# Routing order and filler products at the first expert of a two-stage mixture-of-experts kernel

## The chip, the cores and the metric

One core of a Trainium2 chip runs the whole program as one launch. The metric is device time in microseconds (us) of that launch, lower is better; the times given are medians of several runs on one chip, and the rows come from one further execution that was profiled.

## The reference, cut to what matters

The reference is an attention layer, a first mixture-of-experts layer and a second one (3072 tokens of 512 values, 8 experts, hidden size 1024). The change touches only the second:

```
logits = x @ w_gate                      # 3072 x 8
for idx in argsort(-logits.flatten()):   # best (token, expert) pair first
    tok, e = idx // 8, idx % 8
    if assigned[tok] >= 0 or counts[e] >= 384: continue
    assigned[tok] = e; counts[e] += 1
for e in range(8):
    h = relu(x[assigned == e] @ w1[e])   # 384 rows, 512 -> 1024
    out[assigned == e] = h @ w2[e]       # 1024 -> 512
```

Every expert ends with exactly 384 tokens, but who gets which token depends on all the experts that filled up earlier.

## The kernel before, in words

The expert stages of the second layer are `phase_d` (L911 on); they begin at about 287 us of the profile. The order in which the experts are worked on is found on the chip. One **choice** (`Route2.phase`, L774) finds the next expert to fill: a search in five steps (`NSTEP`) for the logit threshold, each step made of a comparison on VectorE (`p_g`, L801), a count on TensorE (`rt_ps`, L808 for the first choice, L810 for the later ones), a short chain on VectorE (L819 to L822), a sum over partitions on TensorE (L824) and the new threshold (L826). Then come the assignment (L834 to L844), a count (L841), the expert's number `p_ei` (L853, which the weights' load on SyncE waits for) and positions (L857 to L868). **The update** (`Route2.update`, L872) takes the filled expert and the assigned tokens out of the logits (L875 to L878); the next choice begins with it. **The list** (`Route2.list`, L879) turns positions into the 384 row numbers `p_ix` of the expert (L882 to L890 on VectorE and ScalarE, L896 or L899 on TensorE, L906).

With `p_ix` GpSimd gathers the rows: `gather` (L937) issues three indirect DMAs of 128 rows (L941). `fetch` (L917) loads the weights as four 1 MB chunks from SyncE's queue (for the first expert two of them from GpSimd's). `conv` (L920) splits a quarter of a chunk into a high part (ScalarE cast, L925) and a low part (subtraction, L934, on GpSimd; the first four on VectorE). `xT` (L949) turns 128 gathered rows: four TensorE transposes (L952), a cast on ScalarE and a subtraction on VectorE (both L955). `L1` (L956) makes the hidden values: for each of 8 blocks `f`, four groups of three 384-column products (L963 to L965), then ReLU (L968) and the low part (L969). `L2` (L974) makes the result: for each of 3 blocks `b`, eight groups of three 512-column products (L980 to L982), a copy (L985) and the indirect store (L987, issued by GpSimd). So an expert is 56 groups of three products, called **pieces** here: pieces 1 to 32 are L1, 33 to 40, 41 to 48 and 49 to 56 the blocks of L2.

All engines work through their instructions in the order in which the program was written, and that order comes from a planner at the end of `phase_d` that runs when the program is built. It keeps a clock `now`, in modelled us, and a clock `dve` for VectorE. A piece of L1 moves `now` by 0.522, a piece of L2 by 0.7 (what `yield` gives back). The route and the list are generators, too: each step adds its modelled VectorE time to `dve` (`busy`), and the next step is due 0.1 after that (0.25 from the second expert on). Between two pieces `try_thread` (L1013) runs a step that is due, lists first; `housekeeping` (L1037), asked only after an even number of pieces, issues a gather, a fetch or a conversion; `xts_step` (L1050) issues a turn once `now` is 4.5 us past the gather (one more us for each later block) and 34 pieces or more of the running expert are out:

```
if route[0] is None and route[2]<7 and (route[2] in routed if route[2] else 0 in listed): R.update(); busy(1.25); start_route(route[2]+1)
if (curp>=0 or xts.get(0,3)==3 or now[0]<gath_t[0]+HOLD) and try_thread(): continue
h=housekeeping() if hk or cur is None else False
if xts_step(): continue
```

`routed` holds the choices whose search and positions are done, `listed` those whose list is done. So before the change the update and the next choice follow as soon as a choice is routed, with the list's steps among them; only after the first choice (number 0) do they wait for its list. Choice 1 is made while expert 0 is worked on, choice 2 from the second half of expert 0 on.

`warm` (L487) issues products of a constant 128x128 matrix with 512 constant columns (L489), whose result nobody reads. Thirteen of them stand behind the first list (L909). `R.psum()` (L763) is the one PSUM tile of the route, `rt_ps`.

Of the kernel before, what the change touches and what calls it, by code (L numbers as in the profile page):

```python
# [6 lines left out]
F32=mybir.dt.float32; BF=mybir.dt.bfloat16; F32R=mybir.dt.float32r; I32=mybir.dt.int32; U32=mybir.dt.uint32  # L7
# [479 lines left out]
def warm(nc,st,p,n):  # L487

    for _ in range(n): nc.tensor.matmul(p,st['ones_b'],st['it32'].rearrange("p s c->p (s c)")[:,0:512],start=True,stop=True)  # L489
# [421 lines left out]
def phase_d(nc,tc,ctx,I,st,out,R,W,wk,ps,cp):  # L911
# [24 lines left out]
    def busy(x): dve[0]=max(dve[0],now[0])+x  # L936
# [12 lines left out]
    def xT(p,b):  # L949
        if b==0: S[p]['xh']=wk.tile([128,4,CAP],F32R,name="dxh",bufs=1); S[p]['xl']=wk.tile([128,4,CAP],F32R,name="dxl",bufs=1)  # L950
        q=ps.tile([128,512],F32,name="dh_ps",bufs=3).rearrange("p (d c)->p d c",d=4); x=S[p]['x'][b]
        for d in range(4): T.transpose(q[:,d,:],x[:,128*d:128*d+128],ident)  # L952
        c=slice(128*b,128*b+128); h=S[p]['xh'][:,:,c]
        busy(0.72)
        A.copy(h,q); V.tensor_tensor(S[p]['xl'][:,:,c],q,h.bitcast(F32),op=OP.subtract)  # L955
    def L1(p,f):  # L956
        s=S[p]
        if f==0: s['hh']=wk.tile([128,8,CAP],F32R,name="dhh",bufs=1); s['hl']=wk.tile([128,8,CAP],F32R,name="dhl",bufs=1)
        wh,wl=s['w'][f//4]
        q=ps.tile([128,512],F32,name="dh_ps",bufs=3)[:,0:CAP]  # L960
        for d in range(4):
            c=slice(512*d+128*(f%4),512*d+128*(f%4)+128)
            T.matmul(q,wh[:,c],s['xh'][:,d,:],start=(d==0),stop=False)  # L963
            T.matmul(q,wh[:,c],s['xl'][:,d,:],start=False,stop=False)  # L964
            T.matmul(q,wl[:,c],s['xh'][:,d,:],start=False,stop=(d==3))  # L965
            if d<3: yield 0.522
        h=s['hh'][:,f,:]
        A.activation(h,q,AF.Relu)  # L968
        def low(s=s,f=f,q=q,h=h): V.scalar_tensor_tensor(s['hl'][:,f,:],q,0.0,h.bitcast(F32),op0=OP.max,op1=OP.subtract)  # L969
        defer.append((now[0]+0.522+0.5,low))  # L970
        yield 0.522
    def flush(t=1e9):
        while defer and defer[0][0]<=t: busy(0.6); defer.pop(0)[1]()
    def L2(p,b):  # L974
# [16 lines left out]
    def expert(p):  # L991
        for f in range(8): yield from L1(p,f)
        for b in range(3): yield from L2(p,b)


    route=[None,0.0,0]
    pend=[]
    lists=[]
    rdy={}
    routed=[]; listed=[]  # L1000
    def step(th):

        try:
            lat,dur=next(th[0])
        except StopIteration: return False
        busy(lat); th[1]=dve[0]+(0.25 if curp>0 else 0.1); th.append(dur) if len(th)==3 else th.__setitem__(3,dur)
        return True
    def start_route(ph):
        route[0]=R.phase(ph); route[2]=ph; step(route)
# [3 lines left out]
    def try_thread():  # L1013
        for th in lists+[route]:
            if th[0] is not None and now[0]>=th[1]:
                now[0]+=th[3]
                if not step(th):
                    ph=th[2]; th[0]=None
                    if th is route:
                        routed.append(ph); pend.append(ph)  # L1020
                    else:
                        lists.remove(th); listed.append(ph)
                    if pend and not lists:
                        ph=pend.pop(0); l=[R.list(ph),now[0],ph]; lists.append(l); step(l)
                return True
        return False
# [11 lines left out]
    def housekeeping():  # L1038

        q=curp+1  # L1040
        if q==7 and q not in gath_t and q in listed and xts.get(curp)==3: gather(q); gath_t[q]=max(pool[0],now[0]); pool[0]=gath_t[q]+3.1; xts[q]=0; return True
        if curp>=0 and cur is not None and conv_step(curp,(0,0,0,0)): return True
        if q>7: return False
        if q not in fetch_t and q in routed and conved.get(curp,16)==16:
            fetch(q); fetch_t[q]=now[0]; conved[q]=0; return True
        if q not in gath_t and q in listed: gather(q); gath_t[q]=max(pool[0],now[0]); pool[0]=gath_t[q]+3.1; xts[q]=0; return True
        if xts.get(q,3)<3 and 33<=npc<=45: return False
        if cur is None and xts.get(q,0)<3 and conved.get(q,0)>=8: return False
        return conv_step(q,(0,0,18,34) if cur is not None else (0,0,0,0))
    def xts_step():  # L1050
        q=curp+1
        if q<=7 and xts.get(q,3)<3 and now[0]>=gath_t[q]+4.5+1.0*xts[q] and (cur is None or npc>=34+4*xts[q]):
            xT(q,xts[q]); xts[q]+=1; now[0]+=0.45; return True
        return False
    hk=True; HOLD=3.0
    while True:
        flush(now[0])
        if route[0] is None and route[2]<7 and (route[2] in routed if route[2] else 0 in listed): R.update(); busy(1.25); start_route(route[2]+1)
        if (curp>=0 or xts.get(0,3)==3 or now[0]<gath_t[0]+HOLD) and try_thread(): continue
        h=housekeeping() if hk or cur is None else False  # L1060
        if xts_step(): continue
        if cur is not None:
            if npc==32 and conved[curp]<12 or npc==36 and conved[curp]<16:
                hk=True
                if not h: now[0]+=0.3
                continue
            try: now[0]+=next(cur); npc+=1; hk=npc%2==0
            except StopIteration: cur=None
            if cur is not None: continue
            if curp==7: break  # L1070
        if cur is None:
            q=curp+1
            if xts.get(q,0)==3 and conved.get(q,0)>=8:
                curp=q; cur=expert(q); npc=0; continue
            if not h: now[0]+=0.3
# [4 lines left out]
def program(nc,tc,I,out,dbg=None):  # L1080
    with ExitStack() as ctx:
# [34 lines left out]
        ps=ctx.enter_context(tc.tile_pool(name="c_ps",reuse_waits="tile",bufs=2,space=PSUM))  # L1116
        R=Route2(nc,tc,cp,wk,ps,I,st)
        phase_d(nc,tc,ctx,I,st,out,R,W,wk,ps,cp)

# [15 lines left out]
```

## Time and profile before

| | us |
|---|---|
| median of 3 runs (lowest, highest) | 638.8 (638.35, 639.43) |
| the profiled execution, its own time | 643.75 |
| its span, first to last instruction | 642.1 |
| TensorE busy in the span | 588.6 (92%) |
| mean granted clock, share of 2.4 GHz | 0.946 |

The time of the profiled execution is what a row's change is set against; it is 4.95 us above the median of the unprofiled runs. In a row of a timeline the first number is the start in us from the span's beginning, the second how long the instruction, or a run of equal ones, took; in brackets stands how long the engine sat idle before it and what it waited for. In a table by stretches `PEclk` is the granted TensorE clock as a share of 2.4 GHz.

### The profile page before, as it was taken

What the parts mean: (1) busy time and instruction counts of PE and PEld (TensorE: products, weight loads), DVE (VectorE), ACT (ScalarE), POOL (GpSimd) and SP (SyncE); (2) the same over time, 40 slices, a digit from 0 to 9 for tenths busy, and PEclk for the clock granted to TensorE, in tenths of its full rate; (3) what the DMA queues carried; (4) which work ended last, traced back from release to release, by engine and by line L of the source; (5) the groups of instructions that cost most, each with busy time, mean ns of one, the idle gap of its engine ahead of it and who ended that gap; (6) DMA issues with size and microseconds to landing.
All of it is one profiled execution on the core that took longest, in us unless ns stands there. A gap on an engine that the chain in (4) does not pass through costs nothing.

```text
span 642.1 us, 13487 instructions
## 1 busy us (share of the span) xinstructions
PE 588.6 (92%) x4848; PEld 465.5 (73%) x4848; DVE 426.4 (66%) x1618; ACT 328.0 (51%) x740; POOL 364.9 (57%) x401
## 2 busy tenths in 40 slices
PE   7799999898799999983599899999999999999994
PEld 3567667666677777753388588797888879798983
DVE  4678888888878996847857447676777767642110
ACT  5789989784367766400341432543517245363610
POOL 2565555432446879610471653875939488496931
PEclk9899999998899999985779879999999999999998
DMA  8999794282099778000712704518082451854000
GB/s 321 404 380 382 252 350 149 91 306 100 29 366 316 238 248 278 20 10 3 244 69 97 264 1 178 184 62 284 17 294 67 177 171 44 316 195 150 33 17 33
DMA packets 48644, 114.62 MB, mean 179 GB/s; under 512 B 3937, under 2 KB 4705, under 8 KB 48576
## 3 DMA queue, kind: packets, MB, share of 16 engines
q1 hardware_dynamic: 40016, 88.60, 38.3%
q0 software_dynamic: 6208, 20.39, 9.4%
q10 hardware_dynamic: 2352, 4.76, 2.1%
q8 instruction: 39, 0.64, 0.4%
q14 instruction: 29, 0.24, 0.1%
HBM read 99.26 MB, written 14.88 MB: 178 GB/s over the span
## 4 chain that ended last, share of the span: by engine, by line
PE 40%; issue 5%; POOL 3%; DVE 3%; DMA 1%; ACT 1%; POOLq 0%; DVEq 0%; ACTq 0%
PE dh_ps L963 7%; PE dh_ps L964 7%; PE dh_ps L965 6%; PE dz_ps L980 5%; PE dz_ps L982 5%; PE dz_ps L981 5%; POOL wl L934 2%; PE dh_ps L952 2%; DMA xg<-xrows,p_ix 1%; PE rt_ps L810 1%; POOL out_dram L987 1%; DVE p_g L801 1%; PE rt_ps L808 1%; ACT dxh L955 0%; ACT wh L925 0%
## 5 line engine op out<-in xcount | busy, mean ns | idle before, releaser
L934 POOL TENSOR_TENSOR wl<-wraw,wh 128x512 fp32r<-128x512 f32 x124 | 155.6, 1290 | 14.3 <-ACT wh L925 13.9
L963 PE MATMUL dh_ps<-dxh,wh 128*128 128x384 f32 x256 | 94.2, 368 | 2.5 <-ACT dxh L955 2.5
L964 PE MATMUL dh_ps<-dxl,wh 128*128 128x384 f32 x256 | 89.8, 351 | 0.4 <-DVE dxl L955 0.3
L965 PE MATMUL dh_ps<-dxh,wl 128*128 128x384 f32 x256 | 89.0, 348 | 0.0
L980 PE MATMUL dz_ps<-wh,dhh 128*128 128x512 f32 x192 | 78.8, 410 | 0.0
L982 PE MATMUL dz_ps<-wh,dhl 128*128 128x512 f32 x192 | 76.0, 396 | 0.0
L981 PE MATMUL dz_ps<-wl,dhh 128*128 128x512 f32 x192 | 76.0, 396 | 0.0
L925 ACT CAST wh<-wraw 128x512 fp32r<-128x512 f32 x128 | 73.5, 619 | 2.8 <-DMA wraw<-in_w1b_dram 2.8
L968 ACT ACTIVATE dhh<-dh_ps 128x384 fp32r<-128x384 f32 x64 | 31.5, 493 | 84.4 <-PE dh_ps L965 73.3
L987 POOL DMA_INDIRECT out_dram<-dz,io x24 | 24.6, 1025 | 86.8 <-ACT dz L985 84.7
L969 DVE SCALAR_TENSOR_TENSOR dhl<-dh_ps,dhh 128x384 fp32r<-128x384 f32 x64 | 35.5, 555 | 56.0 <-ACT dhh L968 55.9
L133 ACT ACTIVATE p_e<-s_sb,nm 128x118 f32<-128x118 f32 x192 | 59.9, 389 | 0.0
L985 ACT COPY dz<-dz_ps 128x512 f32<-128x512 f32 x24 | 14.1, 587 | 85.4 <-PE dz_ps L982 60.3
L963 PEld LDWEIGHTS dh_ps<-dxh,wh 128*128 128x128 f32 x256 | 50.4, 197 | 3.1 <-ACT dxh L955 2.8
L505 POOL TENSOR_TENSOR wl<-wraw,wh 128x1024 fp32r<-128x1024 f32 (+1 forms) x18 | 37.4, 2106 | 26.6 <-ACT wh L504 26.6
L504 ACT CAST wh<-wraw 128x1024 fp32r<-128x1024 f32 (+1 forms) x56 | 48.9, 932 | 6.3 <-DMA wraw<-in_w1a_dram 6.0
L964 PEld LDWEIGHTS dh_ps<-dxl,wh 128*128 128x128 f32 x256 | 50.3, 196 | 2.3 <-DVE dxl L955 2.2
L965 PEld LDWEIGHTS dh_ps<-dxh,wl 128*128 128x128 f32 x256 | 50.0, 195 | 0.0
L115 POOL COPY VV<-wraw 24x1024 f32<-24x1024 f32 x24 | 24.0, 1032 | 45.6 <-ACT wraw L114 45.6
L505 DVE TENSOR_TENSOR wl<-wraw,wh 128x1024 fp32r<-128x1024 f32 (+1 forms) x38 | 45.0, 1222 | 5.9 <-ACT wh L504 5.9
L127 DVE CUSTOM_DVE_ANT_0 s_sb<-s_ps,cst 128x118 f32<-128x118 f32 x192 | 41.9, 275 | 9.9 <-PE s_ps L123 7.7
L941 POOL DMA_INDIRECT xg<-xrows,p_ix x24 | 23.3, 973 | 38.5 <-DVE rrow L875 24.3
(340 smaller groups left out, 1375.0 us busy)
## 6 DMA issues: line engine op xcount, KB each, us to landing
wraw<-in_w1b_dram SPq DMA_DIRECT2D x16, 1024.0 KB, 6.7
wraw<-in_w2b_dram SPq DMA_DIRECT2D x14, 1024.0 KB
VV<-in_v_dram SPq DMA_DIRECT2D x16, 780.0 KB, 11.7
wraw<-in_w2a_dram SPq DMA_DIRECT2D x12, 1024.0 KB, 9.2
wraw<-in_w1a_dram SPq DMA_DIRECT2D x10, 1024.0 KB
kt<-in_k_dram SPq DMA_DIRECT2D x16, 384.0 KB, 6.3
qd<-in_q_dram SPq DMA_DIRECT2D x16, 384.0 KB, 6.0
wraw<-in_vt_dram SPq DMA_DIRECT2D x8, 768.0 KB, 8.8
```

The costliest lines, as they stand in the source:

```text
L127: V.tensor_tensor_reduce(out=sb[:,j,:],in0=p[j%2][:,j//2,0:118],in1=mk,scale=-0.125,scalar=3e38,op0=OP.add,op1=OP.min,accum_out=nm[:,j:j+1])
L133: A.activation(pe[:,j,:],sb[:,j,:],AF.Exp,bias=nm[:,j:j+1],scale=-1.0)
L504: (hi.tensor_copy if hi else nc.scalar.copy)(h[:,c],t[:,c])
L505: (lo or nc.vector).tensor_tensor(l[:,c],t[:,c],h[:,c].bitcast(F32),op=OP.subtract)
L925: A.copy(h[:,c],t[:,c])
L934: eng.tensor_tensor(l[:,c],t[:,c],h[:,c].bitcast(F32),op=OP.subtract)
L963: T.matmul(q,wh[:,c],s['xh'][:,d,:],start=(d==0),stop=False)
L964: T.matmul(q,wh[:,c],s['xl'][:,d,:],start=False,stop=False)
L965: T.matmul(q,wl[:,c],s['xh'][:,d,:],start=False,stop=(d==3))
L980: T.matmul(q,s['hh'][:,f,c0],wh[:,c],start=(f==0),stop=False)
L981: T.matmul(q,s['hh'][:,f,c0],wl[:,c],start=False,stop=False)
L982: T.matmul(q,s['hl'][:,f,c0],wh[:,c],start=False,stop=(f==7))
```

## The change

Three edits, all in `phase_d`:

- `L1`: for the first expert (`p` is 0) the planner counts 0.65 instead of 0.522 for each piece of the blocks `f` 0 and 1, that is for pieces 1 to 8. No instruction is added.
- A new list `laid` is filled together with `listed`. After choice 1 the update and choice 2 now wait until list 1 is done (`route[2] in laid`), as they did after choice 0. Choices from 2 on are as before.
- `xts_step`: behind the three turns of the first expert's rows (`q==0`) stand 3, 3 and 2 products of constants into `rt_ps`.

```diff
-        q=ps.tile([128,512],F32,name="dh_ps",bufs=3)[:,0:CAP]
+        q=ps.tile([128,512],F32,name="dh_ps",bufs=3)[:,0:CAP]; t=0.522 if p or f>1 else 0.65
...
-            if d<3: yield 0.522
+            if d<3: yield t
...
-        defer.append((now[0]+0.522+0.5,low))
-        yield 0.522
+        defer.append((now[0]+t+0.5,low))
+        yield t
...
-    routed=[]; listed=[]
+    routed=[]; listed=[]; laid=[]
...
-                        lists.remove(th); listed.append(ph)
+                        lists.remove(th); listed.append(ph); laid.append(ph)
...
-            xT(q,xts[q]); xts[q]+=1; now[0]+=0.45; return True
+            xT(q,xts[q]); xts[q]+=1; now[0]+=0.45
+            if q==0: warm(nc,st,R.psum(),(3,3,2)[xts[q]-1])
+            return True
...
-        if route[0] is None and route[2]<7 and (route[2] in routed if route[2] else 0 in listed): R.update(); busy(1.25); start_route(route[2]+1)
+        if route[0] is None and route[2]<7 and (route[2] in routed if route[2]>1 else route[2] in laid): R.update(); busy(1.25); start_route(route[2]+1)
```

## Rows read from the trace of the kernel before

**Rows 1.** The page's part 2, granted TensorE clock in 40 slices of the span

```profile
PEclk9899999998899999985779879999999999999998
```

**Rows 2.** Busy us by stretch: PE, PEld, DVE, ACT, POOL; then PEclk, DMA share, GB/s

```profile
315.00:320.00 5.00, 2.38 (x14) 1.41 (x14) 3.89 (x7) 2.68 (x5) 2.52 (x4) 1.00 0.77 217
320.00:325.00 5.00, 5.00 (x27) 4.54 (x28) 1.81 (x7) 2.58 (x6) 5.00 (x5) 0.57 0.80 282
325.00:330.00 5.00, 5.00 (x32) 4.42 (x31) 2.41 (x8) 1.52 (x3) 1.86 (x2) 0.75 0.02 8
...
355.00:360.00 5.00, 5.00 (x42) 3.90 (x39) 2.18 (x9) 2.57 (x5) 2.31 (x3) 1.00 1.03 395
...
365.00:370.00 5.00, 3.12 (x14) 2.40 (x13) 3.26 (x10) 3.35 (x7) 4.97 (x5) 0.51 0.13 52
...
400.00:405.00 5.00, 5.00 (x49) 3.74 (x48) 2.19 (x9) 0.44 (x1) 2.61 (x3) 1.00 1.02 374
```

**Rows 3.** Timeline of PE, the first expert's turns and its first product

```profile
310.11 4.81 PE L489 MATMUL rt_ps<-it,ones_b 128*128 128x512 bf16 x13
314.82 0.66 PE L952 MATMUL dh_ps<-cb,xg 128*128 128x128 f32 x4
316.38 0.66 PE L952 MATMUL dh_ps<-cb,xg 128*128 128x128 f32 x4 [0.91 <-DMA xg<-xrows,p_ix]
317.79 0.66 PE L952 MATMUL dh_ps<-cb,xg 128*128 128x128 f32 x4 [0.75 <-DMA xg<-xrows,p_ix]
319.13 0.45 PE L963 MATMUL dh_ps<-dxh,wh 128*128 128x384 f32 x1 [0.67 <-ACT dxh L955]
```

**Rows 4.** Timeline of PE, products of the first expert at either clock

```profile
320.96 0.52 PE L963 MATMUL dh_ps<-dxh,wh 128*128 128x384 f32 x1
...
327.61 0.34 PE L965 MATMUL dh_ps<-dxh,wl 128*128 128x384 f32 x1
...
332.11 0.34 PE L965 MATMUL dh_ps<-dxh,wl 128*128 128x384 f32 x1
...
333.13 0.34 PE L964 MATMUL dh_ps<-dxl,wh 128*128 128x384 f32 x1
```

**Rows 5.** Timeline of PE, second half of expert 0 and all of expert 1's L1

```profile
343.67 0.40 PE L980 MATMUL dz_ps<-wh,dhh 128*128 128x512 f32 x1
...
362.18 0.40 PE L982 MATMUL dz_ps<-wh,dhl 128*128 128x512 f32 x1
363.92 0.66 PE L952 MATMUL dh_ps<-cb,xg 128*128 128x128 f32 x4 [1.35 <-DMA xg<-xrows,p_ix]
...
368.79 0.69 PE L963 MATMUL dh_ps<-dxh,wh 128*128 128x384 f32 x1 [1.84 <-ACT dxh L955]
...
393.06 0.39 PE L980 MATMUL dz_ps<-wh,dhh 128*128 128x512 f32 x1
```

**Rows 6.** Timeline of DVE, list 1 and choice 2 among its steps

```profile
349.19 0.19 DVE L883 TENSOR_SCALAR st_ps<-st_ps 128x24 int32<-128x24 int32 x1
...
350.62 0.36 DVE L780 TENSOR_REDUCE st_ps<-Lm 128x24 f32<-128x192 f32 x1
...
355.61 0.64 DVE L906 SCALAR_TENSOR_TENSOR p_ix<-st_ps,l_oc 32x3 int32<-32x3 f32 x4
```

**Rows 7.** Timeline of POOL, the gather of expert 1's rows

```profile
357.08 1.00 POOL L987 DMA_INDIRECT out_dram<-dz,io  x1 [4.76 <-ACT dz L985]
358.39 1.00 POOL L941 DMA_INDIRECT xg<-xrows,p_ix  x1 [0.30 <-issue]
```

**Rows 8.** Timelines of POOL and PE, from expert 1 to expert 2

```profile
402.87 1.01 POOL L941 DMA_INDIRECT xg<-xrows,p_ix  x1 [2.08 <-DVE p_ix L906]
...
408.68 0.66 PE L952 MATMUL dh_ps<-cb,xg 128*128 128x128 f32 x4
409.10 0.47 PE L980 MATMUL dz_ps<-wh,dhh 128*128 128x512 f32 x1
...
413.20 0.42 PE L963 MATMUL dh_ps<-dxh,wh 128*128 128x384 f32 x1
```

## The prediction

> **What bounds the kernel now.** I read the page's 40 slices first. TensorE is busy nearly everywhere and its clock is near full, with dips around slices 19 to 24 [rows 1], and that is where the changed code runs. The table by stretches of 5 us then says what is wrong there: the clock is full from 315 to 320 while TensorE is busy for only 2.38 of 5 us, 0.57 and 0.75 of full in the next two stretches although TensorE is busy throughout, and again 0.51 from 365 to 370 [rows 2]. So two things cost time: products at half clock at the start of each of the first two experts, and a hole between them. From 380 us on TensorE works without a gap to the last result, so what the first two experts lose or win should reach the end.
>
> The timeline of TensorE explains the first dip. Thirteen products of constants bring the clock up; then come three turns, each waiting for its gather, and the expert's first product at 319.13 [rows 3]. In that stretch TensorE was more than half idle, and from about 320.7 on the products stand 0.32 us apart (1.2 GHz) instead of 0.177 (2.4 GHz) until 327.61 [rows 4].
>
> The hole: expert 0's last product starts at 362.18, the first turn for expert 1 waits for the gathered rows until 363.92, expert 1 begins at 368.79 and its L1 lasts to 393.06, 24.27 us, much of it at half clock [rows 5, 2]. The gather is late for two reasons. List 1 is stretched: between its second instruction (349.19) and its last (355.61) VectorE also does the update and begins choice 2 [rows 6]. And on GpSimd's queue the gather stands behind the store of expert 0's second block, which waits for that block: 357.08, then the gather at 358.39, though `p_ix` was complete at 356.25 [rows 6, 7]. One expert later the same hand-over works: gather at 402.87, turns from 408.68 inside the old expert's L2, next expert at 413.20, no hole [rows 8].
>
> **The change, part by part.** *Products of constants.* Eight of 512 columns; between the turns TensorE waits anyway. At full clock each takes at most 0.26 us (expert 0's L2, 72 products of the same width and four small blocks, took 18.9 us [rows 5]); the thirteen, mostly at half clock, took 0.37 each [rows 3]. The gaps are wide enough: the first turn ends at 315.48, three products end by 316.26, the next turn came at 316.38; the last turn ends at 318.45, two products end by 318.97, the first L1 product came at 319.13 [rows 3]. Cover: the wait for gather, cast and subtraction; without it they would cost 2.1 us at the one and 3 us at the other price. Benefit: if TensorE stays busy enough to keep its clock, the stretch 320.96 to 327.61 (17 products, one L810 block, one L824) takes 17 x 0.177 + 0.67 + 0.13 = 3.8 us instead of 6.65. The 0.67 is 332.11 to 333.13 less two product spacings [rows 4]; the 0.13 is an estimate from the same timeline. **Gain 2.85**; bounds 0 (the clock falls all the same) and 2.85.
>
> *The planner's 0.65.* No instruction; it moves route steps earlier in TensorE's order. I walked the planner's clocks through expert 0 with it: the five counts come after pieces 3, 9, 14, 19, 25 instead of 4, 10, 15, 21, 26, and choice 1 ends after piece 39 instead of 40. Could TensorE then wait for VectorE at a count? The gaps between sum and next count stay at 3 pieces (1.6 us) or more, and threshold and comparison take 1.3 us, so I count 0, at most 0.3 for each of five counts.
>
> *List before update.* The list's steps now go out after pieces 39, 40, 43, 44 and end after 46; before, 40, 41, 46, 47 and 50. Piece 48 carries the second block's store, so at 46 the gather goes on GpSimd's queue **ahead** of it. Update and choice 2 come behind the list on VectorE; queued behind them are only choice 2's counts, which the planner places later too: after pieces 53 and 56. The store now waits behind three gather issues (some 3.9 us of GpSimd); nobody needs it soon. In `p_ix` time: 356.25 less three pieces of 0.7 is about 354.1 against 358.39 now, so the gather is 4.3 us earlier relative to TensorE's work. A gather took from 358.39 to just before 363.92, 5.5 us [rows 5, 7]; landing is then about 15.9 us behind the start of L2, and the planner puts the turns after pieces 53, 53 and 54, 15.8 us behind it. So they fit inside L2, with a wait of 0 to 2 us; I take 0.5.
>
> Expert 0's L2 lasted 18.9 us (343.67 to 362.58). Add three turns at 0.42 [rows 8] and one more count (0.67): 20.8, plus 0.5 wait, 21.3 to expert 1's start, against 25.12 now [rows 5]. **Gain 3.8**; bounds 2.3 and 4.4.
>
> *Expert 1 at full clock.* With no hole nothing lowers the clock (expert 2 started so [rows 8]). 96 x 0.177 + 3 x 0.67 + 4 x 0.13 is 19.5 us instead of 24.27. **Gain 4.75**; bounds 0 (a hole remains) and 4.75.
>
> *Later.* By the walk, choice 2 ends after piece 35 of expert 1, as before, with both clocks in the same relation, so the order from there on is the old one and the gain is carried to the end.
>
> Sum: 2.85 + 3.8 + 4.75 = 11.4. Against the profiled execution: 643.75 - 11.4 = 632.35 (span 630.7); the unprofiled median lies 4.95 lower, so 627.4.
>
> One thing speaks against the moved gather. It now goes out while the weights are still coming: DMA share 1.03 from 355 to 360 [rows 2], instead of at their end. The Trainium skill (DMA: Bandwidth & Descriptors, "Issuing engines are not separate DMA queues") says that transfers issued from different engines run on the same 16 DMA engines and interleave; by that the gather and the weights delay each other. 0.79 MB of rows at 395 GB/s is an estimate of 2.0 us, which would make the sum 9.9. The hand-over in rows 8 shows turns 5.8 us behind a gather that also began while the share was 1.02 (400 to 405 [rows 2]), so I stay with 0.5.
>
> **Rivals.** *The clock falls all the same.* For: it fell after a stretch that held turns, which the change keeps. Against: eight products fill the waits. Then 2.85 is lost, the order is unchanged: 630.3. Chance 0.2.
>
> *The list ends one piece later.* Its last two due times meet `now` exactly: 0.6 + 0.1 is one piece of 0.7, 1.3 + 0.1 is two. If rounding breaks a tie, it ends after 47, the gather is asked for after 48, behind the store, as now. Then only the first gain is left: 636. Chance 0.06.
>
> *Choice 2 never catches up (slower).* Place: update and choice 2 behind list 1. If choice 2 ends after piece 38 instead of 35 of expert 1, its gather falls behind piece 48's store and the hole comes again, at 4.4 + 4.75 = 9 us a time. It decides from the second such hand-over; choices follow each other without slack, so all five up to expert 6 would have it: 638.8 - 11.4 + 5 x 9 = 672. Against: the walk gives piece 35. Chance 0.06.
>
> *The gather and the weights collide* by the 2 us above or more, in part of the hand-over: 630. Chance 0.08.
>
> **How the numbers follow.** Forecast as summed: chance 0.6, 627.4. About 0.2% (1.3 us) is what a measurement can tell from no change. Faster takes in the forecast, the fallen clock, the collision and most of the late list: 0.91; slower 0.06; same 0.03. The range: below, the sum of the upper bounds (12.0) and some 2 us for cold stretches that differ between executions, 624.5; above, the fallen clock with the collision's 2 us and a little, 633.5. That leaves out the late list and the slow case, and some of the unprofiled spread.
>
> **What would show it.** Right: the clock stays full from 314 us to the end; L810 first comes after nine L1 products; L2 of expert 0 begins near 340.8; the gather is issued by GpSimd ahead of the second block's store, near 351; three turns lie inside expert 0's L2; expert 1 begins near 362 and its L1 lasts 19.5 us. Wrong: clock at 0.5 behind 320; the gather behind the store; L952 waiting over 2 us; a hole at a later hand-over.

## The result, and the profile after

| | before | after |
|---|---|---|
| median of 11 runs each, us (lowest, highest) | 639.43 (637.9, 642.82) | 633.83 (632.26, 637.2) |
| the profiled execution, its own time, us | 643.75 | 636.16 |
| its span, us | 642.1 | 634.4 |

The changed kernel is faster: ratio 0.9908, 95% interval 0.9886 to 0.993; the medians lie 5.6 us apart. The forecast was 627.4 us with a range of 624.5 to 633.5. So the direction is right and the size is half of what was forecast. The time lies just above the range. Of all the runs told of here one lies far off, 794.89 us at a mean granted clock of 0.646 (old order with products, e5), and no ratio below includes it.

The first view of after is the page's second part, the granted clock of TensorE in 40 slices [rows 1]:

```profile
PEclk8689999979799999995599999999999999999998
```

The dips that stood behind slice 20 are gone. The one in slices 19 and 20 lies ahead of the first expert's turns, where [rows 1] have it too. In slices 1 to 3, 9 and 11, which the change doesn't touch, the clock is lower than in [rows 1]. Next the same view as [rows 2], busy us by stretch of 5 us (PE, PEld, DVE, ACT, POOL, then the granted clock, the DMA share, GB/s):

```profile
315.00:320.00 5.00, 4.51 (x22) 2.17 (x21) 4.83 (x11) 2.30 (x5) 4.33 (x6) 0.91 0.84 251
320.00:325.00 5.00, 4.18 (x30) 2.72 (x29) 2.58 (x6) 3.06 (x6) 2.40 (x2) 1.00 0.93 295
325.00:330.00 5.00, 5.00 (x38) 4.42 (x39) 3.35 (x13) 3.48 (x7) 5.00 (x5) 1.00 0.32 125
...
355.00:360.00 5.00, 4.62 (x20) 3.38 (x18) 2.94 (x7) 2.15 (x4) 4.12 (x7) 1.00 1.05 398
360.00:365.00 5.00, 3.94 (x33) 3.08 (x34) 2.91 (x9) 2.92 (x6) 4.30 (x4) 1.00 0.34 132
365.00:370.00 5.00, 5.00 (x47) 4.19 (x45) 3.46 (x11) 3.88 (x8) 3.81 (x6) 1.00 0.15 56
```

From 320 us on the clock is full, through the first expert's L1 and through the hand-over to the second, where [rows 2] had 0.57, 0.75 and 0.51. TensorE's timeline shows what stands between the turns now [rows 3]:

```profile
313.71 3.62 PE L489 MATMUL rt_ps<-it,ones_b 128*128 128x512 bf16 x11 [0.22 <-issue]
317.70 0.66 PE L952 MATMUL dh_ps<-cb,xg 128*128 128x128 f32 x4 [0.37 <-DMA xg<-xrows,p_ix]
318.19 0.81 PE L489 MATMUL rt_ps<-it,ones_b 128*128 128x512 bf16 x3
319.12 0.66 PE L952 MATMUL dh_ps<-cb,xg 128*128 128x128 f32 x4
319.61 0.81 PE L489 MATMUL rt_ps<-it,ones_b 128*128 128x512 bf16 x3
320.72 0.66 PE L952 MATMUL dh_ps<-cb,xg 128*128 128x128 f32 x4 [0.29 <-DMA xg<-xrows,p_ix]
321.21 0.59 PE L489 MATMUL rt_ps<-it,ones_b 128*128 128x512 bf16 x2
322.05 0.45 PE L963 MATMUL dh_ps<-dxh,wh 128*128 128x384 f32 x1 [0.24 <-ACT dxh L955]
...
343.67 0.47 PE L980 MATMUL dz_ps<-wh,dhh 128*128 128x512 f32 x1
...
360.59 0.66 PE L952 MATMUL dh_ps<-cb,xg 128*128 128x128 f32 x4 [0.97 <-DMA xg<-xrows,p_ix]
...
363.49 0.18 PE L824 MATMUL rt_ps<-p_any,ones_b 128*128 128x1 bf16 x1 [0.46 <-DVE p_any L822]
...
365.96 0.45 PE L963 MATMUL dh_ps<-dxh,wh 128*128 128x384 f32 x1
...
385.76 0.39 PE L980 MATMUL dz_ps<-wh,dhh 128*128 128x512 f32 x1
```

The products are hidden as forecast: they take the place of most of the idle time that stood ahead of the second and third turn (0.91 and 0.75 us before, none and 0.29 now) and of the first product (0.67 before, 0.24 now). The lower rows are the hand-over. The first turn now starts 16.92 us after L2's start at 343.67, inside L2, and it waits 0.97 us for its gathered rows. Inside the hand-over the sum over partitions of choice 2 (L824) waits 0.46 us for VectorE. Expert 1 begins at 365.96 with no idle time in front of it, where [rows 5] had 1.84 us. GpSimd's timeline answers to [rows 7], VectorE's to [rows 6]:

```profile
354.36 1.03 POOL L941 DMA_INDIRECT xg<-xrows,p_ix  x1 [2.16 <-DVE rrow L875]
...
358.42 1.08 POOL L987 DMA_INDIRECT out_dram<-dz,io  x1 [0.21 <-issue]
```

```profile
348.44 0.19 DVE L883 TENSOR_SCALAR st_ps<-st_ps 128x24 int32<-128x24 int32 x1
...
353.44 0.64 DVE L906 SCALAR_TENSOR_TENSOR p_ix<-st_ps,l_oc 32x3 int32<-32x3 f32 x4
...
355.32 0.36 DVE L780 TENSOR_REDUCE st_ps<-Lm 128x24 f32<-128x192 f32 x1
```

The gather stands ahead of the second block's store on GpSimd's queue, 4.06 us ahead of it, where it stood behind. On VectorE the list is done (353.44) before choice 2 begins (355.32). From its second instruction to its last it takes 5.00 us, against 6.42 in [rows 6].

So each step of the forecast is in the trace; the hand-over, 22.29 us from 343.67 to 365.96, is 1.0 us longer than forecast. Where is the other half of the gain? The sum of the three stretches that were forecast (expert 0's L1, the hand-over, expert 1's L1) fell from 73.93 us [rows 3, 5] to 385.76 - 322.05 = 63.71, by 10.2. That is near the forecast's 11.4. All expert stages, from the first use of the logits (L727 on VectorE, 287.02 us before, 289.79 after) to the end of the span, fell from 355.05 to 344.57, by 10.5. Of that, 2.8 were lost again because the stages began later, in phases that the change doesn't touch. The profiled execution of before lay above all 11 runs of the same kernel in the table, though (643.75 against a median of 639.43). The experiments had to tell whether its cold stretches were ordinary.

### The profile page after: what moved, and what is told of

The parts are those of the page before. It is cut to its first block, busy times and chain, and to the rows that moved or that the text cites. A ratio compares the mean times of both kernels' runs of the same rounds, so it can differ in the third digit from the quotient of the medians.

```text
span 634.4 us, 13501 instructions
## 1 busy us (share of the span) xinstructions
PE 585.2 (92%) x4853; PEld 462.7 (73%) x4856; DVE 424.2 (67%) x1618; ACT 328.4 (52%) x740; POOL 363.6 (57%) x401
## 4 chain that ended last, share of the span: by engine, by line
PE 41%; issue 4%; POOL 3%; DVE 3%; DMA 2%; ACT 0%; POOLq 0%; DVEq 0%; ACTq 0%
PE dh_ps L963 7%; PE dh_ps L964 6%; PE dh_ps L965 6%; PE dz_ps L980 6%; PE dz_ps L981 6%; PE dz_ps L982 6%; POOL wl L934 2%; PE dh_ps L952 2%; DMA xg<-xrows,p_ix 2%; PE rt_ps L810 1%; DVE p_g L801 1%; PE rt_ps L808 1%; POOL out_dram L987 1%; PE dx_ps L896 0%; PE rt_ps L824 0%
## 5 line engine op out<-in xcount | busy, mean ns | idle before, releaser
L963 PE MATMUL dh_ps<-dxh,wh 128*128 128x384 f32 x256 | 91.3, 357 | 0.2 <-ACT dxh L955 0.2
L964 PE MATMUL dh_ps<-dxl,wh 128*128 128x384 f32 x256 | 87.2, 340 | 0.3 <-DVE dxl L955 0.3
L965 PE MATMUL dh_ps<-dxh,wl 128*128 128x384 f32 x256 | 86.4, 338 | 0.0
L980 PE MATMUL dz_ps<-wh,dhh 128*128 128x512 f32 x192 | 78.8, 410 | 0.0
L964 PEld LDWEIGHTS dh_ps<-dxl,wh 128*128 128x128 f32 x256 | 48.2, 188 | 1.9 <-DVE dxl L955 1.8
L963 PEld LDWEIGHTS dh_ps<-dxh,wh 128*128 128x128 f32 x256 | 48.4, 189 | 1.0 <-ACT dxh L955 0.7
L965 PEld LDWEIGHTS dh_ps<-dxh,wl 128*128 128x128 f32 x256 | 48.1, 188 | 0.0
L505 DVE TENSOR_TENSOR wl<-wraw,wh 128x1024 fp32r<-128x1024 f32 (+1 forms) x38 | 42.8, 1164 | 5.3 <-ACT wh L504 5.3
```

The source lines that it names most:

```text
L505: (lo or nc.vector).tensor_tensor(l[:,c],t[:,c],h[:,c].bitcast(F32),op=OP.subtract)
L980: T.matmul(q,s['hh'][:,f,c0],wh[:,c],start=(f==0),stop=False)
```

## The experiments

In all of them three distances are read from TensorE's timelines, from the first L963 or L980 row of each: **L1 of 0** is from expert 0's first product to its L2, **hand-over** from there to expert 1's first product, **L1 of 1** from there to its L2. **Stages** is from the L727 row to the end of the span, to about 0.05 us, since a span is given to a tenth.

| kernel | L1 of 0 | hand-over | L1 of 1 | stages | their start |
|---|---|---|---|---|---|
| before, the profile of the forecast | 24.54 | 25.12 | 24.27 | 355.05 | 287.0 |
| before, second (e1) | 22.89 | 24.59 | 21.71 | 350.08 | 288.7 |
| before, third (e7) | 22.94 | 24.48 | 21.79 | 350.10 | 288.1 |
| after, first | 21.62 | 22.29 | 19.80 | 344.57 | 289.8 |
| after, second (e8) | 21.60 | 22.36 | 19.79 | 344.49 | 286.8 |
| after, third (e11) | 21.60 | 22.12 | 19.79 | 344.25 | 287.5 |
| products alone (e2) | 21.58 | 24.16 | 20.23 | 346.85 | 287.4 |
| list first with 0.65, no products (e3) | 21.60 | 22.44 | 19.79 | 344.39 | 290.1 |
| the same again (e10) | 21.60 | 22.34 | 19.78 | 344.45 | 288.4 |
| 0.65 alone (e9) | 24.59 | 23.87 | 21.59 | 350.23 | 284.9 |
| list first and products, without 0.65 (e4) | 21.56 | 23.45 | 23.85 | 383.03 | 288.9 |
| old order, products at both experts (e5) | 21.58 | 24.64 | 20.23 | 347.44 | 287.8 |
| after, two chunks behind the gather (e6) | 21.62 | 21.11 | 19.79 | 343.32 | 290.1 |
| the same again (e12) | 21.60 | 21.10 | 19.79 | 342.76 | 285.6 |

### The kernel before, twice more

No edit.

> The kernel before, unchanged, profiled once more. Theory 1 (the profiled execution of before was unusually slow at the hand-over to expert 1: the clock was low there for 13.7 us, other executions lose less): from the start of expert 0's L2 to the start of expert 1's L2 this execution takes 44 to 46 us instead of 49.4, and the clock is low for 3 to 7 us there. Theory 2 (the stretch is always 49 us, and what the change wins there is lost outside the expert stages): again 49 us and the clock low for 10 us or more.

> The kernel before a third time. The first profile took 73.9 us from the start of expert 0's L1 to the start of expert 1's L2, the second 69.2. If the first was the rare one: 68 to 71 us here. If it was the usual one: 73 us or more.

The two executions took 640.68 and 640.02 us. The table by stretches of e1, columns as above:

```profile
320.00:325.00 5.00, 4.04 (x15) 3.42 (x13) 1.78 (x3) 2.66 (x5) 3.66 (x3) 0.66 0.96 351
325.00:330.00 5.00, 5.00 (x47) 4.56 (x47) 3.32 (x13) 2.96 (x6) 3.55 (x4) 1.00 0.12 47
...
365.00:370.00 5.00, 2.62 (x13) 2.04 (x14) 3.68 (x10) 3.22 (x7) 4.97 (x5) 0.89 0.13 52
370.00:375.00 5.00, 5.00 (x33) 4.58 (x32) 1.35 (x8) 0.49 (x1) 3.45 (x3) 0.77 0.01 3
375.00:380.00 5.00, 5.00 (x38) 4.58 (x38) 3.40 (x11) 3.04 (x6) 3.05 (x3) 1.00 0.00 0
```

The granted clock has two levels here, 2.4 GHz and half of it (1.00 and 0.50 in the stretches that hold one alone), so a stretch of 5 us with a share c held 2 x (1 - c) x 5 us at the lower one. Behind the turns that makes 3.4 us here (0.66), where [rows 2] make 4.3 + 2.5 = 6.8 (0.57 and 0.75). At the hand-over it is 1.1 + 2.3 = 3.4 us. The third execution has 3.4 us behind the turns as well (0.66) and 3.4 at the hand-over (0.83 and 0.83). In the first one the 0.51 of [rows 2] was only the beginning: the next two stretches have

```profile
370.00:375.00 5.00, 5.00 (x26) 4.56 (x25) 1.39 (x3) 0.49 (x1) 3.45 (x3) 0.50 0.00 0
375.00:380.00 5.00, 5.00 (x21) 4.59 (x19) 2.45 (x8) 1.45 (x3) 0.37 (x1) 0.63 0.02 3
```

which makes 4.9 + 5.0 + 3.7 = 13.6 us. So the instructions and their order are the same, and the clock falls at the same two places, though not at the same moment: at the hand-over it fell at about 365.1 in the first execution, ahead of expert 1's first product (368.79 [rows 5]), and at about 368.9 in e1, just behind it (368.27). How long it stays low differs, too: the stages of the first execution are 355.05 - 350.09 = 4.96 us longer than those of the other two. From the start of expert 0's L2 to that of expert 1's, e1 took 46.3 us, just above theory 1's 44 to 46 and well below the 49 of theory 2; e7 took 69.2 us for the longer stretch, as expected if the first execution was the rare one.

### The kernel after, twice more

No edit.

> The changed kernel a second time. The first profile took 63.7 us for the same stretch with the clock full all through. If the eight products hold the clock in any execution: 63.5 to 64.2 us. If it was luck: the clock low for 3.4 us or more somewhere in the stretch and 65 us or more.

> The changed kernel, timed beside the next one. 5 to 6 us below before, ratio 0.990 to 0.992; in the profile 63.5 to 64.0 us from the start of expert 0's L1 to the start of expert 1's L2.

One execution of 633.05 us, and then a median of 634.43 with a ratio of 0.992 (0.9893 to 0.9947), 4.6 us below the median of before in the same series (639.02), where 5 to 6 were expected. The three profiles of after agree within some 0.3 us in every column but the start of the stages. The gain against the two later profiles of before is 350.09 - 344.44 = 5.65 us, near the 5.6 of the first medians and within the interval of both series.

### The products of constants alone

Before, with only this edit:

```diff
-            xT(q,xts[q]); xts[q]+=1; now[0]+=0.45; return True
+            xT(q,xts[q]); xts[q]+=1; now[0]+=0.45
+            if q==0: warm(nc,st,R.psum(),(3,3,2)[xts[q]-1])
+            return True
```

> Only the eight products of constants; planner costs and list as before. If their gain is the clock of expert 0's L1: L1 of expert 0 21.6 to 22 us instead of 24.5, the clock full from 314 us to the hand-over, time 2.5 to 3 us below before. If the products only fill the waits and the clock falls all the same: L1 24 us or more, time within 1 us of before. The hole before expert 1 stays in both.

Median 638.47, ratio 0.9982 (0.9958 to 1.0006): a gain of about 1 us that isn't told from none, where 2.5 to 3 were expected. In the profile L1 of expert 0 took 21.58 us, as expected and as with the whole change. The old hole was there, and yet the clock stayed full after it:

```profile
360.00:365.00 5.00, 2.33 (x25) 1.82 (x25) 2.00 (x8) 4.63 (x9) 4.79 (x6) 1.00 0.35 119
365.00:370.00 5.00, 4.50 (x32) 3.98 (x33) 2.95 (x9) 0.66 (x2) 5.00 (x5) 1.00 0.01 3
```

TensorE's timeline has the hole here with the same instructions in it as in e1, and nearly as long. The first two rows are e1's, its first turn of expert 1 and its first product; the last two are those of this run:

```profile
363.84 0.66 PE L952 MATMUL dh_ps<-cb,xg 128*128 128x128 f32 x4 [1.25 <-DMA xg<-xrows,p_ix]
368.27 0.44 PE L963 MATMUL dh_ps<-dxh,wh 128*128 128x384 f32 x1 [1.42 <-ACT dxh L955]
```

```profile
360.78 0.66 PE L952 MATMUL dh_ps<-cb,xg 128*128 128x128 f32 x4 [0.82 <-DMA xg<-xrows,p_ix]
365.22 0.44 PE L963 MATMUL dh_ps<-dxh,wh 128*128 128x384 f32 x1 [1.42 <-ACT dxh L955]
```

In e1 the clock fell just behind it and here it did not. So neither the hole's instructions nor how busy TensorE is in it settles by itself whether the clock falls.

### The order alone, twice

After, without the products:

```diff
-            if q==0: warm(nc,st,R.psum(),(3,3,2)[xts[q]-1])
```

> Only the order: list 1 ahead of the update and the 0.65 of the planner, no products. Theory 1: the hole shrinks as in the changed kernel (L2 of expert 0 to L1 of expert 1 22 to 22.5 us), L1 of expert 0 stays at 24 to 24.5, and the time is 2.5 to 3 us below before, since in most executions the hole and its cold stretch cost only that much. Theory 2: 7 to 8 us below before in the stages and in the time.

> The order without products a second time. In the first profile the clock stayed full in L1 of expert 0 (21.60 us) though no products stood between the turns. If that was the luck of one execution: the clock low for 3.4 us or more behind the turns and L1 22.9 to 24.5 us here. If the order alone keeps the clock: 21.6 us again.

Median 635.41, ratio 0.9933 (0.9898 to 0.9968), a gain of 4.0 us, between the two theories; the second execution took 634.6. The hand-over came out as with the whole change (22.44 and 22.34). L1 of expert 0 was a miss: it took 21.60 us in both, not the 24 or so that was expected of a clock that falls behind the turns. The table by stretches of e3:

```profile
315.00:320.00 5.00, 4.88 (x18) 2.10 (x16) 4.71 (x12) 2.13 (x4) 4.36 (x6) 0.65 0.83 261
320.00:325.00 5.00, 3.38 (x26) 2.62 (x27) 3.13 (x6) 3.25 (x6) 2.74 (x3) 1.00 0.88 270
```

In this execution the clock came back only after some 3.5 us of the first stretch (0.65), at about 318.5, just as the turns began (the first at 318.62, the first product of L1 at 322.00), and then it stayed. In e10 it came back at about 315.6 and stayed, too, with the first product of L1 at 320.44:

```profile
315.00:320.00 5.00, 3.23 (x18) 1.67 (x16) 4.31 (x8) 1.36 (x3) 3.22 (x5) 0.94 0.65 181
320.00:325.00 5.00, 4.27 (x31) 3.60 (x32) 2.63 (x8) 3.39 (x8) 4.01 (x4) 1.00 0.98 343
```

Whether it was the program or the execution that kept it is answered by the next kernel.

### The planner's 0.65 alone

After without the products, and with the condition of before:

```diff
-        if route[0] is None and route[2]<7 and (route[2] in routed if route[2]>1 else route[2] in laid): R.update(); busy(1.25); start_route(route[2]+1)
+        if route[0] is None and route[2]<7 and (route[2] in routed if route[2] else 0 in listed): R.update(); busy(1.25); start_route(route[2]+1)
```

> Only the 0.65 of the planner for the first eight pieces; no products, and the update follows choice 1 at once, as before. Choice 1 then ends after piece 39, but its list, with update and choice 2 among its steps, after 49, and the gather is issued after piece 50, behind the store, as before. If the place of the gather on GpSimd's queue makes the gain: the hand-over stays at 24 to 25 us and the time within 1.5 us of before. If the earlier counts alone do it: 22.5 us and 3 us below before.

Median 637.31, ratio 0.9976 (0.9954 to 0.9999), 1.7 us below before. GpSimd's timeline still has the old order,

```profile
354.43 1.00 POOL L987 DMA_INDIRECT out_dram<-dz,io  x1 [4.76 <-ACT dz L985]
355.74 1.00 POOL L941 DMA_INDIRECT xg<-xrows,p_ix  x1 [0.30 <-issue]
```

so the 0.65 alone doesn't bring the gather forward. (Nor does the list's place alone, as the next kernel shows: it takes both.) The hand-over (23.87) came out a little shorter than expected. By stretches:

```profile
310.00:315.00 5.00, 3.38 (x16) 1.54 (x14) 4.62 (x10) 2.21 (x5) 4.15 (x5) 0.93 0.81 236
315.00:320.00 5.00, 3.90 (x17) 2.97 (x17) 2.47 (x4) 2.67 (x6) 2.98 (x3) 0.75 0.91 294
320.00:325.00 5.00, 5.00 (x28) 4.67 (x27) 2.15 (x7) 1.97 (x4) 4.02 (x4) 0.57 0.29 118
```

The clock fell behind the turns for 2.5 + 4.3 = 6.8 us and L1 of expert 0 took 24.59, as in the forecast's profile. This kernel and the order alone (e3, e10) give every engine the same instructions in the same order up to the later steps of list 1, in the middle of expert 0's L2. The one lost its clock in L1 and the others did not. So at this place, without the products, it is the single execution and not the program that decides. Counted over the study: without products between the turns the clock fell in L1 of expert 0 in 4 of 6 profiles (before three times, e9; not in e3, e10), with them in none of 8.

The granted clock also tells when it came up, at the thirteen products: at about 310.7 here (0.93), 5.8 us ahead of L1's first product at 316.48. In the other three that lost it later it came up 5.3 (before), 6.5 (e1) and 6.5 us (e7) ahead of that product, in the two that kept it without products 3.5 (e3) and 4.8 us (e10). So when the clock came up differed from execution to execution, and this goes with what happened; that it decides isn't shown. With products between the turns it came up 5.8 to 6.5 us ahead in four profiles (after, e2, e5, e6) and 4.7 to 5.0 in the other four, and stayed in all. At 5.3 to 6.5 us, then, it fell in four of four without them and in none of four with them, the clearest sign here that the products keep it.

### List first and products, without the 0.65

After, with the planner's old cost:

```diff
-        q=ps.tile([128,512],F32,name="dh_ps",bufs=3)[:,0:CAP]; t=0.522 if p or f>1 else 0.65
+        q=ps.tile([128,512],F32,name="dh_ps",bufs=3)[:,0:CAP]; t=0.522
```

> The changed kernel without the 0.65: list 1 ahead of the update, products kept. The planner then ends choice 2 after piece 38 of expert 1, and every later gather up to expert 6's is issued after piece 50, behind the store of piece 48. The slow rival of the prediction: a hole at five hand-overs of 4.4 us each, with the clock down after it 9 us each, so 22 to 45 us above the changed kernel. The other theory: the holes are shorter than expert 1's, because later choices give TensorE work in them and the clock stays: 1 to 2 us each, 5 to 10 us above the changed kernel.

Median 672.65, ratio 1.0493 (1.0441 to 1.0544): slower by 33 us than before. The time is that of the forecast's slow rival, 672, but the agreement of the price is luck. The rival kept the first hand-over's gain and lost 9 us at each of five later ones. In the run all six gathers stand behind their stores, the first one too (store at 355.89, gather at 357.20, though the list was done at 353.64), and the stages are 383.03 - 344.44 = 38.6 us longer than after's, 6.4 us on average at each of six. GpSimd's timeline at the third hand-over:

```profile
447.03 0.96 POOL L987 DMA_INDIRECT out_dram<-dz,io  x1 [4.86 <-ACT dz L985]
448.30 1.00 POOL L941 DMA_INDIRECT xg<-xrows,p_ix  x1 [0.30 <-issue]
```

and TensorE's:

```profile
454.56 0.66 PE L952 MATMUL dh_ps<-cb,xg 128*128 128x128 f32 x4 [0.81 <-DMA xg<-xrows,p_ix]
457.57 0.69 PE L963 MATMUL dh_ps<-dxh,wh 128*128 128x384 f32 x1 [2.35 <-ACT dxh L955]
```

The gather is again behind the store, the turns come after L2, and the expert's first products run at half clock. By stretches:

```profile
455.00:460.00 5.00, 2.50 (x13) 1.57 (x12) 3.16 (x8) 2.52 (x5) 4.97 (x5) 0.61 0.13 52
...
500.00:505.00 5.00, 3.05 (x13) 2.35 (x14) 2.88 (x10) 1.74 (x4) 4.98 (x5) 0.55 0.13 52
```

The same dip comes at each of the six hand-overs behind experts 0 to 5. So the 0.65, which adds no instruction and alone is worth little, decides here whether the whole change wins 5.6 us or loses 33. The three edits can't be priced one by one and added.

### The old order with products in the hole

Before, with products at both experts' turns:

```diff
+            P=lambda: ps.tile([128,512],F32,name="dx_ps",bufs=1)
+            if q==1 and xts[q]==0: warm(nc,st,P(),5)
-            xT(q,xts[q]); xts[q]+=1; now[0]+=0.45; return True
+            xT(q,xts[q]); xts[q]+=1; now[0]+=0.45
+            if q==0: warm(nc,st,R.psum(),(3,3,2)[xts[q]-1])
+            if q==1: warm(nc,st,P(),(2,2,6)[xts[q]-1])
+            return True
```

> Order and costs as before (the hole before expert 1 stays), but products of constants at the turns of expert 0 and also of expert 1: five ahead of the first turn, then 2, 2 and 6. If the lost time at expert 1 is partly the clock after the hole: the clock is full from the first list to the end, L1 of expert 1 takes 19.8 to 20.3 us in every execution, the hand-over stays at 24 to 24.6, and the time lies 1.5 to 3 us below that of the products at expert 0 alone (638.5), that is 635.5 to 637. If only the hole itself counts: 638 to 639.

Median 637.01, ratio 0.9937 (0.9912 to 0.9961). The hole stays (24.64 us of hand-over) and the clock stays full through it (L1 of expert 1 takes 20.23). In the stages that leaves 347.44 - 344.44 = 3.0 us for the order, 2.3 of it in the hand-over, and 350.09 - 347.44 = 2.65 us for the clock. That the products in the hole kept the clock isn't shown: e2 kept it there without them, with the same 20.23 and stages of 346.85, by which the order is worth 2.4 us.

### Two more chunks of weights behind the gather

After, and expert 1's third and fourth chunk are asked for only after the gather of its rows has been issued, and then from GpSimd's queue instead of SyncE's, as those of expert 0 already are:

```diff
-        S.setdefault(p,{}).update(raw=[load_chunk(W,w1,w2,e,j) for j in range(4 if 'x' in S.get(p,()) else 2 if p==0 else 4)],w={})
+        S.setdefault(p,{}).update(raw=[load_chunk(W,w1,w2,e,j) for j in range(4 if 'x' in S.get(p,()) else 2 if p<=1 else 4)],w={})
```

> The changed kernel, but the last two of expert 1's four weight chunks are loaded from GpSimd's queue behind the gather, as expert 0's are. If the gather shares the DMA engines with the weights, it lands 1 to 2 us earlier, the first turn no longer waits 0.97 us, L2 of expert 0 to L1 of expert 1 takes 20.8 to 21.5 us instead of 22.29, and the time falls by 0.5 to 1.5 us. If the weights are not what it waits for: 22.3 us again and the time within 0.5 us of the changed kernel (633.8), or above it, since two more loads go through GpSimd's queue.

> The changed kernel with two of expert 1's weight chunks loaded behind the gather, timed beside it. If the 1.2 us that the hand-over won in its first profile is there in every execution: 0.8 to 1.5 us below the changed kernel, hand-over 21.0 to 21.3 us. If it was one execution's: within 0.5 us of it.

The gather on GpSimd's timeline of e6, the stretch behind it, and TensorE's timeline:

```profile
354.44 1.02 POOL L941 DMA_INDIRECT xg<-xrows,p_ix  x1 [2.18 <-DVE rrow L875]
```

```profile
355.00:360.00 5.00, 5.00 (x25) 3.95 (x23) 3.01 (x7) 2.14 (x4) 4.24 (x7) 1.00 0.54 152
```

```profile
359.55 0.60 PE L952 MATMUL dh_ps<-cb,xg 128*128 128x128 f32 x4
...
364.86 0.44 PE L963 MATMUL dh_ps<-dxh,wh 128*128 128x384 f32 x1
```

The first turn no longer waits. It starts 5.11 us behind its gather (issued at 354.44), where it was 6.23 in after, and the hand-over is 21.11, 1.2 us shorter; the second execution says 21.10. The DMA share behind the gather, from 355 to 360, is 0.54 where it was 1.05 in after. So what delayed the gathered rows was weights that were on their way at the same time. The Trainium skill (DMA: Bandwidth & Descriptors, "Issuing engines are not separate DMA queues") says that transfers issued from different engines run on the same 16 DMA engines and interleave. The trace agrees with it: with two of the four chunks out of the way the gather took 5.11 us or less instead of 6.23. The forecast estimated 2.0 us for the collision; half of the weights made 1.2, and what the other half costs wasn't tried. The times were 633.97 (0.9891, 0.9854 to 0.9927) and 632.8 (0.9901, 0.9865 to 0.9936). In the second case this is 1.6 us below after in the same series, but the intervals overlap, so only the profile tells this version, which has the lowest median of the study, from after.

## Why the prediction was wrong, step by step

*The products of constants*: the mechanism held. They are hidden, and the clock stayed full through expert 0's L1 in all eight profiles that had them. L1 of expert 0 took 21.6 us, as forecast (24.54 - 2.85 = 21.7). The term of 2.85 was mis-sized: against 22.9 in the two later profiles of before it is 1.3. The rival of the fallen clock did not come.

*The planner's 0.65*: cost nothing that shows, as forecast. What the prediction doesn't say is that the rest hangs on it: the run without it (e4) has the gather behind the store at all six hand-overs. The rivals of the late list and of the slow choice had a gather behind the store, but as a slip of the walk and not as what the 0.65 prevents.

*List before update*: right in its order. List, gather and turns lie where the walk through the planner's clocks put them. The hand-over was forecast at 21.3 and took 22.3. The mis-sized term is the wait of 0.5. The work in it (L2, three turns, one count) was 22.29 - 0.97 - 0.46 = 20.86, forecast 20.8; the two waits were 1.43, forecast 0.5. Here the choice was wrong: the hand-over in [rows 8] was taken as the measure for a gather among weights, and the collision, which had a rival of its own at 2.0 us, was there with 0.97 us (1.2 us came back in e6 and e12). The gather went out 10.69 us behind L2's start, against some 10.4 forecast; the wait of L824 for VectorE was not foreseen.

*Expert 1 at full clock*: right, 19.8 us against 19.5 forecast. The term of 4.75 was mis-sized: against the 21.75 of the later profiles of before it is 1.95.

*Later*: right. No hole came at a later hand-over: from expert 1's L2 on every L1 and every hand-over of after is within 0.25 us of before's, so the gain is carried to the end.

*The sum against the profiled execution*: this is the step that failed. It took 11.4 from 643.75 and then a further 4.95, "the unprofiled median lies 4.95 lower", as if that difference would remain. But the difference is what the change removes: the profiled execution of before had 6.8 + 13.6 us at the lower clock in these stretches and the two later ones 3.4 + 3.4, which makes their stages 4.96 us shorter. The same 5 us were counted twice, once as gain and once as a lower start. These 4.95, the 1.0 of the hand-over and the 0.6 by which the median of before came out higher (639.43 against 638.8) lead from 627.4 to 634.0, where 633.83 was measured. With the terms of the later profiles (1.3, 24.54 - 22.29 = 2.25 and 1.95) the sum is 5.5, the measured gain 5.6. The range did allow for "cold stretches that differ between executions", but it put those 2 us at its lower end; they belonged at the upper one.

**What stays open.** When the clock came up goes with whether it falls behind the turns without products, in six profiles; that this decides wasn't tried. How much of the gain the products bring once the order is changed isn't settled either: order alone 4.0 us (2.0 to 6.5), the whole change 5.6 (4.5 to 7.3), and both profiles of the order alone kept the clock, with the shortest times from its return to L1's first product among those without products.

## What to carry to other kernels

A term that is read from a cold stretch is a term of one execution: before such terms are added up, the same kernel should be profiled again, and where the profiled execution is some us above the median, ask first whether the difference lies in the very stretches that the change is to mend. In an order that a planner writes, a cost of 0.13 us that adds no instruction can decide which of two transfers goes first on a queue; try such an edit with and without it. A gather that stands ahead of a store in the queue can still be slowed by weights on their way; asking for half of them behind it gave back 1.2 us.

## What the runs showed of the hardware that was not expected

With the same instructions in the same order the lower clock lasted 6.8 us in one execution and 3.4 us in two others behind the first turns, and 13.6 against 3.4 at the first hand-over. Two programs that are alike up to there once lost the clock behind the turns (e9) and twice kept it (e3, e10).

The phases ahead of the expert stages, which no kernel here touches, ended anywhere from 284.9 to 290.1 us in the profiles. The mean granted clock goes with a part of that. In the table by stretches the rows of the first 280 us are, for e9 and then for the first profile of after,

```profile
0.00:280.00 280.00, 258.18 (x2845) 188.78 (x2847) 219.75 (x890) 194.21 (x474) 156.44 (x192) 0.98 0.68 243
```

```profile
0.00:280.00 280.00, 259.25 (x2825) 190.65 (x2827) 219.22 (x887) 193.97 (x473) 153.21 (x189) 0.95 0.68 243
```

with stages that begin at 284.9 and at 289.8. It isn't all: e12 begins at 285.6 with a clock of 0.96. So part of the scatter between the runs of one kernel (before: 637.9 to 642.82) can come from the clock in stages that the change doesn't touch, and a comparison of the stages alone, from profiles, tells differences of 1 us that the times of whole runs did not, as long as the clock does the same in both.
